# The last batch's routing and the first expert's token rows put in another order in an attention and mixture-of-experts kernel

## The chip, the cores and the metric

The kernel runs on one core of a Trainium2 chip. The metric is the device time of one execution in microseconds (us). The engines are PE (TensorE), DVE (VectorE), ACT (ScalarE), POOL (GpSimd) and SP (SyncE, which here only issues DMAs and loads numbers).

## The reference, cut to what matters

Attention with two masks gives rows of tokens; each row whose skip score is positive then goes through one of eight experts, the one with the largest gate logit.

```python
batch, n_heads, seq, head_dim = (8, 8, 576, 64)
N, D, E, F = (4608, 512, 8, 1024)
...
mask_local = (rel >= 0) & (rel < stride)
mask_strided = (rel >= 0) & (pos[None, :] % stride == pos[:, None] % stride)
masks = np.stack([mask_local if h < H // 2 else mask_strided for h in range(H)], axis=0)
...
return np.matmul(attn, v).astype(np.float32)
...
skip_score = x @ w_skip
do_compute = skip_score > 0
out = x.copy()
xc = x[do_compute]
logits = xc @ w_gate
e_idx = np.argmax(logits, axis=1)
...
for e in range(E):
    mask = e_idx == e
    h = np.maximum(xc[mask] @ w1[e], 0.0)
    y[mask] = gate_w[mask, None] * (h @ w2[e])
out[do_compute] = xc + y
```

## The kernel before

**Attention.** The work comes in 32 units, one for each batch (0 to 7) and quarter `pr` (0 to 3); the quarters 0 and 1 take the heads with the local mask, 2 and 3 the strided ones. The loop over the units stands under a manual schedule of POOL, PE, DVE and SP, so that these engines run what they are given in the order in which the code is written. Finished rows `x` are stored to `out` in DRAM.

**Routing.** Batches form groups (two and two first, then single ones). For each group `score` makes skip score and logits on PE (L381) and copies them to the tile `s9s` (four copies on ACT, L386). `route1` turns them (L400 on PE) and finds each token's expert: a chain on DVE (L408 to L423), the exponentials on ACT (L412), and on POOL the sums and the mask `rmk` of the tokens that are skipped (L428 to L432). `route2` gives each token its place in its expert's list: counting products on PE (L441 to L448), then DVE (L453 to L458, of which L457 needs `rmk`). `scat` writes these places by indirect DMAs on POOL into a `table` in DRAM (L470, five for a group of one batch). What is scattered waits in the list `sc_`. After the last group, `sort` and `places` count the experts' tokens (from L483 on PE, L488 to L543 on DVE) and leave the sorted numbers of the experts and their first rows in `order`.

**The experts.** Products are made of two float32r parts each (high `h`, low `l`), three products for one. The first expert, "e", is picked early, after batch 3, with 96 by 3 rows from batches up to 5. `rows` fetches its rows of the table into `tab` (a DMA, L638, on POOL or on SP), `gather` fetches the token rows `xg` from `out` (three indirect DMAs on POOL, L650), `xturn` turns them on PE (L675) and splits them on ACT (L677, `xh`) and DVE (L678, `xl`). `ffn1a` makes the hidden rows of the first two of eight blocks f (16 products with `xh`, L720, then eight with `xl`, L724), `ffn1` those of the others (L681 to L683), each block ended by `hout` (ACT L693, DVE L694). `ffn2` is the second layer: weights 0 to 3 of `w2` are called j 4 to 7, and its second half needs j 6 and 7. A weight tile comes by a DMA of 512 KB on SP (`wdma`, L596) into one of three `raw` tiles, is cast on ACT (L610) and its low part taken on DVE (L615).

Behind "e" come a leftover chunk "l" of 128 rows (turned at L675, products L788 to L815) and the other seven experts in sorted order, the first of which the code calls TURN[0]. Their table rows are read by `rows` on SP with numbers that SP loads out of `order` one by one. Which of two versions of the expert loop runs is decided by a branch on a number that `places` makes; the traced execution ran one. The transposes, the first products of "e", the routing of the last batch and the sorting stand in a manual schedule of PE, ACT and DVE; POOL and SP are ordered there by a scheduler.

Of the kernel before, what the change touches and what calls it, by code (L numbers as in the profile page):

```python
# [104 lines left out]
def attn_moe(ctx: ExitStack, tc: tile.TileContext, q, k, vl, vh, vs, w9d, w1d, w2d, cst, out, NB=B):  # L105
# [265 lines left out]
    def score(b, tag="T"):  # L371
# [13 lines left out]
        for h in range(4):  # L385
            A.copy(s9s[:, at + SQT * h:at + SQT * h + SQT], p[32 * h:32 * h + 9, 0:SQT])  # L386

# [451 lines left out]
    def run(*gs):  # L839
        weave(gs, [])  # L840
# [33 lines left out]
    for n, (b, pr) in enumerate(units):  # L874
# [86 lines left out]
        if b == CB + 2:  # L961
            if pr == 0:
                assert not sc_
            if pr == 1:
                rows("e", s0, *CE, eng=G)
            if pr == 3:
                gather("e", "e", "e", last=(CB + 1) * S)
    pool_order.close()
    nr = len(GROUPS) - 1
    with tc.manual_schedule(engines={T.engine, A.engine, V.engine}):  # L970
        run(pv(*units[-1]), xpose(*units[-2]), route2(ranked, of=CB))
        count(CB)
        run(xpose(*units[-1]), score(NB - 1), xturn("e"))
    while sc_:
        scat(*sc_.pop(0))
    for kind in range(2):
# [6 lines left out]
    ga = ffn1a("e")  # L983
    with tc.manual_schedule(engines={T.engine, A.engine, V.engine}):
        run(ga)
        wsplit("e", 3, 4)
        wdma("e", e0, 6, 7, st_["e"]["taken"])
        g = ffn1("e", 2, 6)
        run(islice(g, 4), later(route1, nr), islice(g, 4), later(route2, nr))
        while sc_:  # L990
            scat(*sc_.pop(0))
        wsplit("e", 4, 5)
        places = sort(NB - 1)
        run(g)
        judge, rest = places()
        actx.close()
        pool["b"] = ctx.enter_context(tc.tile_pool(name="bpool", bufs=1, reuse_waits="tile"))
        wsplit("e", 5, 6)
        run(ffn1("e", 6, 8))
    pctx.close()  # L1000
    psum, bufs = ctx.enter_context(tc.tile_pool(name="psumB", bufs=1, space=PSUM, reuse_waits="tile")), {"S": 4, "T": 2, "PV": 2}

    seq = [("e", e0, 6), ("e", e0, 7)]
    wdma(*seq[1], 8)
    s0n = G.value_load(isel[0:1, 2:3], min_val=0, max_val=(NE - 1) * ESTR + CE[0] * CE[1])
    rows("l", s0n, CT, 1, eng=G)
    slots = {}
    for r in TURN:
        e = nc.sync.value_load(order[0:1, 0, r:r + 1], min_val=0, max_val=NE - 1)
        seq += [(r, e, j) for j in range(8)]  # L1010
        if r == TURN[0]:
            wdma(*seq[2], 1)
        slots[r] = nc.sync.value_load(order[0:1, 1, r:r + 1], min_val=0, max_val=(NE - 1) * ESTR)
        if r == TURN[0]:
            assert SMALL[r] == CAPS[r]
            rows(r, slots[r], *CAPS[r])
    done = [0]

    def split():
        key, _, j = seq[done[0]]  # L1020
        wsplit(key, j, j + 1)
        done[0] += 1
        if done[0] + 2 < len(seq):
            wdma(*seq[done[0] + 2], seq[done[0] + 2][2] + 1)

# [28 lines left out]
    def experts(caps, tm):  # L1054
        last = ("e", CE[1])
        for r in TURN[1:]:
            rows(r, slots[r], *caps[r])
        with tc.manual_schedule(engines={T.engine, A.engine, V.engine, G.engine}):
            for i, r in enumerate(TURN):
                nxt = TURN[i + 1] if i + 1 < len(TURN) else None  # L1060
                if nxt is not None:
                    gather(nxt, "bbe"[(i + 1) % 3], "eh"[(i + 1) % 2])
                g = ffn1(r, 0, 8)
                for f in range(8):
# [114 lines left out]
```

## Time and profile before

| | us |
|---|---|
| median of three runs | 444.77 |
| lowest and highest | 444.13, 451.11 |
| the profiled execution | 448.78 |
| its span, first to last instruction | 447.1 |
| PE busy in it | 407.3 (91%) |
| DVE, ACT, POOL busy | 254.1, 192.8, 153.5 |

The profiled execution is 1.7 us longer than its span, and 4.0 above the median. Its mean granted clock of PE is 0.95 of full speed. An engine's busy time is an average over stages that differ: the attention fills the first 180 us, the experts the rest.

### The profile page before, as it was taken

How to read it: one execution, taken by the hardware profiler on the slowest of the kernel's cores; microseconds unless marked ns; L12 is line 12 of the kernel's file. 1: busy time of each engine (PE TensorE's matmuls, PEld its weight loads, DVE VectorE, ACT ScalarE, POOL GpSimd, SP SyncE). 2: the span in 40 equal slices, each digit the busy share in tenths (PEclk: the TensorE clock that was granted, in tenths of full speed). 3: DMA queues.
4: the chain of work that ended last, by engine and by line, in shares of the span. 5: the costliest groups of instructions: out<-in, count | busy, mean ns of one | idle time of the engine just before them, and what ended most of it. 6: DMA issues, size and time to landing. Idle time of an engine off the chain costs nothing. (4 is left out here: it accounts for less than half of the span.)

```text
span 447.1 us, 12291 instructions
## 1 busy us (share of the span) xinstructions
PE 407.3 (91%) x4995; PEld 365.0 (82%) x4996; DVE 254.1 (57%) x498; ACT 192.8 (43%) x372; POOL 153.5 (34%) x199
## 2 busy tenths in 40 slices
PE   6889998989898978599889999999999999999993
PEld 3778877677675856389779999999999998999973
DVE  4776774567765746265146546446457474757610
ACT  1556472536352715233253344345354454546500
POOL 2443435644748574424401441212202211321011
PEclk9989996999989868799989999999999999999998
DMA  8989998999979415714515866656547565685301
GB/s 270 370 287 296 305 326 181 257 268 271 247 204 286 134 59 139 216 48 96 170 58 160 226 200 180 190 150 199 190 142 227 169 202 173 196 285 162 119 21 46
DMA packets 47440, 86.36 MB, mean 193 GB/s; under 512 B 8095, under 2 KB 24735, under 8 KB 47374
## 3 DMA queue, kind: packets, MB, share of 16 engines
q1 hardware_dynamic: 41262, 75.32, 56.4%
q0 software_dynamic: 6112, 10.17, 7.6%
q8 instruction: 41, 0.67, 0.6%
q14 instruction: 25, 0.20, 0.2%
HBM read 70.44 MB, written 15.39 MB: 192 GB/s over the span
## 5 line engine op out<-in xcount | busy, mean ns | idle before, releaser
L681 PE MATMUL S<-xh,w1h 128*128 128x342 f32 (+5 forms) x248 | 76.6, 309 | 0.8 <-DVE hl L694 0.8
L761 POOL DMA_INDIRECT out_dram<-ot,tab x23 | 24.6, 1068 | 150.2 <-DVE ot L759 139.1
L682 PE MATMUL S<-xl,w1h 128*128 128x342 f32 (+5 forms) x248 | 75.1, 303 | 0.0
L683 PE MATMUL S<-xh,w1l 128*128 128x342 f32 (+5 forms) x248 | 75.0, 302 | 0.0
L681 PE MATMUL S<-hh,w2h 128*128 128x288 f32 (+4 forms) x160 | 50.1, 313 | 0.0
L693 ACT ACTIVATE hh<-S 128x342 fp32r<-128x342 f32 (+5 forms) x64 | 27.1, 425 | 52.9 <-PE S L683 40.7
L615 DVE TENSOR_TENSOR w1l<-raw,w1h 128x1024 fp32r<-128x1024 f32 x32 | 38.7, 1223 | 18.4 <-ACT w1h L610 17.2
L683 PE MATMUL S<-hh,w2l 128*128 128x288 f32 (+4 forms) x160 | 49.0, 306 | 0.0
L682 PE MATMUL S<-hl,w2h 128*128 128x288 f32 (+4 forms) x160 | 49.0, 306 | 0.0
L681 PEld LDWEIGHTS S<-xh,w1h 128*128 128x128 f32 x248 | 46.9, 189 | 1.6 <-DVE hl L694 1.3
L615 DVE TENSOR_TENSOR w2l<-raw,w2h 128x1024 fp32r<-128x1024 f32 x32 | 39.0, 1223 | 14.3 <-ACT w2h L610 10.1
L682 PEld LDWEIGHTS S<-xl,w1h 128*128 128x128 f32 x248 | 46.9, 189 | 0.2
L683 PEld LDWEIGHTS S<-xh,w1l 128*128 128x128 f32 x248 | 46.8, 189 | 0.0
L205 PE MATMUL S<-kt,qt 64*64 64x54 f32 (+1 forms) x1280 | 34.7, 250 | 8.9 <-DVE sm L223 3.2
L470 POOL DMA_INDIRECT table<-pay,rdi x38 | 38.7, 1018 | 10.7 <-issue 9.3
L205 PEld LDWEIGHTS S<-kt,qt 64*64 64x64 f32 x1280 | 28.7, 146 | 14.9 <-issue 8.4
L650 POOL DMA_INDIRECT xg<-out_dram,tab x23 | 27.9, 1215 | 34.1 <-DMA out_dram<-ot,tab 10.0
L232 POOL TENSOR_TENSOR sm<-sm,mx 128x384 f32<-128x384 f32 (+1 forms) x30 | 27.5, 939 | 33.3 <-DVE mx L229 17.9
L694 DVE SCALAR_TENSOR_TENSOR hl<-S,hh 128x342 fp32r<-128x342 f32 (+5 forms) x64 | 29.7, 468 | 16.0 <-ACT hh L693 15.1
L610 ACT CAST w2h<-raw 128x1024 fp32r<-128x1024 f32 x32 | 33.3, 1043 | 2.4 <-DMA raw<-in_w_dram 2.4
L678 DVE TENSOR_TENSOR xl<-T,xh 128x256 fp32r<-128x256 f32 (+6 forms) x30 | 12.6, 451 | 37.6 <-ACT xh L677 26.6
L610 ACT CAST w1h<-raw 128x1024 fp32r<-128x1024 f32 x32 | 33.3, 1060 | 0.0
(161 smaller groups left out, 857.8 us busy)
## 6 DMA issues: line engine op xcount, KB each, us to landing
raw<-in_w_dram SPq DMA_DIRECT2D x64, 512.0 KB
vt<-in_vs_dram SPq DMA_DIRECT2D x16, 390.0 KB
qt<-in_qp_dram SPq DMA_DIRECT2D x16, 304.0 KB
kt<-in_kp_dram SPq DMA_DIRECT2D x16, 297.0 KB
kt<-in_kp_dram SPq DMA_DIRECT2D x14, 304.0 KB
vt<-in_vl_dram SPq DMA_DIRECT2D x16, 260.0 KB
out_dram<-x SPq DMA_DIRECT2D x16, 256.0 KB
qt<-in_qp_dram SPq DMA_DIRECT2D x14, 288.0 KB
```

The costliest lines, as they stand in the source:

```text
L205: mark[0] = T.matmul(s[HP * (i ^ j):HP * (i ^ j) + HP, j, (blk - b0) * win:(blk - b0 + 1) * win], lhsT=qt[p, j, blk * nq:blk * nq + HP], r ...
L232: (V if b == kind == 0 and j else G).tensor_tensor(e[:, j], sw[:, j], mx[:, j].unsqueeze(2).broadcast_to([128, b1 - b0, win]), op=ALU.subt ...
L470: i = G.indirect_dma_start(out=table, out_offset=bass.IndirectOffsetOnAxis(ap=di[:, t:t + 1], axis=0), in_=pay[:, t, :], in_offset=None, b ...
L610: A.copy(hi, raw)
L615: V.tensor_tensor(lo, raw, hi.bitcast(F32), op=ALU.subtract)
L650: i = G.indirect_dma_start(out=xg[:s["P"], t, :], out_offset=None, in_=out[0:last, :], in_offset=bass.IndirectOffsetOnAxis(ap=s["tab"][:s[ ...
L681: T.matmul(p, lhsT=a[0], rhs=b[0], start=start, stop=False)
L682: T.matmul(p, lhsT=a[0], rhs=b[1], start=False, stop=False)
L683: T.matmul(p, lhsT=a[1], rhs=b[0], start=False, stop=stop)
L693: A.activation(s["hh"][:, f, :C], p[:, :C], AF.Relu)
L694: V.scalar_tensor_tensor(s["hl"][:, f, :C], p[:, :C], 0.0, s["hh"][:, f, :C].bitcast(F32), op0=ALU.max, op1=ALU.subtract)
L761: i = G.indirect_dma_start(out=out, in_=ot[:P], in_offset=None, bounds_check=NTOK - 1, oob_is_err=False, out_offset=bass.IndirectOffsetOnA ...
```

## The change

The four copies of the last batch's scores go to DVE. "e"'s token rows are gathered one unit sooner. POOL joins the manual schedules behind the loop. The last batch's `route1` comes between the two halves of "e"'s transposes, its `route2` between the products with `xh` and those with `xl`, and its scatters, the sorting and `places` come before and between the next blocks. TURN[0]'s table row is read on SP before the last two weight tiles of "e" are fetched, and the other experts' numbers are loaded by `load`, called where a weight tile or table row needs them.

```diff
 def score(b, tag="T"):
-            A.copy(s9s[:, at + SQT * h:at + SQT * h + SQT], p[32 * h:32 * h + 9, 0:SQT])
+            (A.copy if b + 1 < NB else V.tensor_copy)(s9s[:, at + SQT * h:at + SQT * h + SQT], p[32 * h:32 * h + 9, 0:SQT])
...
-            if pr == 3:
+            if pr == 2:
                 gather("e", "e", "e", last=(CB + 1) * S)
...
-    with tc.manual_schedule(engines={T.engine, A.engine, V.engine}):
+    with tc.manual_schedule(engines={T.engine, A.engine, V.engine, G.engine}):
         run(pv(*units[-1]), xpose(*units[-2]), route2(ranked, of=CB))
+        while sc_:
+            scat(*sc_.pop(0))
         count(CB)
-        run(xpose(*units[-1]), score(NB - 1), xturn("e"))
-    while sc_:
-        scat(*sc_.pop(0))
+        run(xpose(*units[-1]), score(NB - 1), xturn("e", 0, 2))
+        r1 = route1(nr)
+        next(r1)
+        run(xturn("e", 2, 4), r1)
...
-    with tc.manual_schedule(engines={T.engine, A.engine, V.engine}):
-        run(ga)
+    slots, es = {}, {}
+
+    def load(r, n):
+        x = nc.sync.value_load(order[0:1, n, r:r + 1], min_val=0, max_val=(NE - 1) * (1, ESTR)[n])
+        (es, slots)[n][r] = x
+
+    with tc.manual_schedule(engines={T.engine, A.engine, V.engine, G.engine}):
+        run(islice(ga, 8), later(route2, nr), ga)
+        while sc_:
+            scat(*sc_.pop(0))
+        places = sort(NB - 1)
+        g = ffn1("e", 2, 6)
+        run(islice(g, 4))
+        judge, rest = places()
+        load(TURN[0], 1)
+        assert SMALL[TURN[0]] == CAPS[TURN[0]]
+        rows(TURN[0], slots[TURN[0]], *CAPS[TURN[0]])
         wsplit("e", 3, 4)
         wdma("e", e0, 6, 7, st_["e"]["taken"])
-        g = ffn1("e", 2, 6)
-        run(islice(g, 4), later(route1, nr), islice(g, 4), later(route2, nr))
-        while sc_:
-            scat(*sc_.pop(0))
+        run(islice(g, 4))
         wsplit("e", 4, 5)
-        places = sort(NB - 1)
         run(g)
-        judge, rest = places()
...
-    seq = [("e", e0, 6), ("e", e0, 7)]
-    wdma(*seq[1], 8)
+    es["e"] = e0
+    seq = [("e", 6), ("e", 7)] + [(r, j) for r in TURN for j in range(8)]
+
+    def ahead(n):
+        key, j = seq[n]
+        if key not in es:
+            load(key, 0)
+        wdma(key, es[key], j, j + 1)
+
+    ahead(1)
     s0n = G.value_load(isel[0:1, 2:3], min_val=0, max_val=(NE - 1) * ESTR + CE[0] * CE[1])
     rows("l", s0n, CT, 1, eng=G)
-    slots = {}
-    for r in TURN:
-        e = nc.sync.value_load(order[0:1, 0, r:r + 1], min_val=0, max_val=NE - 1)
-        seq += [(r, e, j) for j in range(8)]
-        if r == TURN[0]:
-            wdma(*seq[2], 1)
-        slots[r] = nc.sync.value_load(order[0:1, 1, r:r + 1], min_val=0, max_val=(NE - 1) * ESTR)
-        if r == TURN[0]:
-            assert SMALL[r] == CAPS[r]
-            rows(r, slots[r], *CAPS[r])
+    ahead(2)
...
-        for r in TURN[1:]:
+
+        def fetch(r):
+            load(r, 1)
             rows(r, slots[r], *caps[r])
+
+        fetch(TURN[1])
         with tc.manual_schedule(engines={T.engine, A.engine, V.engine, G.engine}):
             for i, r in enumerate(TURN):
...
+                if i + 2 < len(TURN):
+                    fetch(TURN[i + 2])
```

**POOL, from the table rows of "e" to the scatters of batch 6's group.** L638 fetches the table rows, L650 gathers `xg`, L428 to L432 are `route1`'s and L470 the scatters. Before:

```order
L638 DMA tab<-table 96x12
L428 TENSOR_TENSOR rex<-rex 128x5x4
L428 TENSOR_TENSOR rex<-rex 128x5x2
L429 TENSOR_TENSOR rz<-rex 128x5
L430 TENSOR_SCALAR rz<-rz 128x5
L432 TENSOR_SCALAR rmk<-rmw 128x5
L650 DMA xg_3205<-out_dram,tab 96x512 x3
L470 DMA table<-pay_94,rdi 40960x4 x5
```

and now:

```order
L638 DMA tab<-table 96x12
L650 DMA xg_3126<-out_dram,tab 96x512 x3
L428 TENSOR_TENSOR rex<-rex 128x5x4
L428 TENSOR_TENSOR rex<-rex 128x5x2
L429 TENSOR_TENSOR rz<-rex 128x5
L430 TENSOR_SCALAR rz<-rz 128x5
L432 TENSOR_SCALAR rmk<-rmw 128x5
L470 DMA table<-pay_94,rdi 40960x4 x5
```

The three gathers stand ahead of that group's L428 to L432 instead of behind them. After these scatters follow, before and now, L428 to L432 of the last group, its five L470 and the reading of "l"'s table rows (L638).

**PE, from the last batch's scores to the first products of "e".** `xg` are the gathered rows, `s9s` the last batch's scores. Before:

```order
L381 MATMUL T<-xT_3101,w_65 32x144 x8
L381 MATMUL T<-xT_3243,w_65 32x144 x8
L675 MATMUL T<-cs,xg_3205 128x96 x12
L720 MATMUL S<-xh_3310,w1h_2859 128x288
L720 MATMUL S<-xh_3310,w1l_2863 128x288
```

and now:

```order
L381 MATMUL T<-xT_3243,w_65 32x144 x8
L675 MATMUL T<-cs,xg_3126 128x96 x6
L400 MATMUL T<-cs,s9s 128x9 x5
L675 MATMUL T<-cs,xg_3126 128x96 x6
L720 MATMUL S<-xh_3325,w1h_2859 128x288
L720 MATMUL S<-xh_3325,w1l_2863 128x288
```

The five L400, which stood behind block f=2, stand between two halves of the twelve L675. In the same way the counting products L441 to L448, which stood behind block f=3, now stand between the last L720 and the eight L724.

**SP, around the weight tiles j 6 and j 7 of "e".** raw_2550 and raw_2551 are the raw tiles that take them, raw_2552 the third (first j 5, then j 0 of TURN[0]); the names in brackets are the engines and DMA lanes whose semaphores the instruction waits for (DMASW: the indirect and other DMAs that POOL issued). Before:

```order
L596 DMA raw_2550<-in_w_dram 128x1024 [waits DMAHW7_49,DVE_49]
L596 ISA
L596 DMA raw_2551<-in_w_dram 128x1024 [waits DMAHW0_49,DVE_49]
L1009 TENSOR_LOAD order [waits DVE_49]
L1009 ISA x2
L596 ISA
L596 DMA raw_2552<-in_w_dram 128x1024 [waits DMAHW6_49,DMAHW1_49,DVE_49]
L1013 TENSOR_LOAD order
L1013 ISA x2
L638 ISA
L638 DMA tab<-table 114x12 [waits DMASW5_49,DMASW4_49,DMASW6_49,DMASW3_49,DMASW7_49,DMASW2_49,DMAHW2_49,DMASW1_49,DMASW0_49]
```

and now:

```order
L596 DMA raw_2552<-in_w_dram 128x1024 [waits DMASW7_49,DMASW6_49,DMAHW6_49,DMASW5_49,Activation_49]
L990 TENSOR_LOAD order [waits DVE_49]
L990 ISA x2
L638 ISA
L638 DMA tab<-table 114x12 [waits DMASW5_49,DMASW4_49,DMASW6_49,DMASW3_49,DMASW7_49,DMASW2_49,DMAHW7_49,DMASW1_49,DMASW0_49]
L596 ISA
L596 DMA raw_2550<-in_w_dram 128x1024 [waits DMAHW0_49,DVE_49]
L596 ISA
L596 DMA raw_2551<-in_w_dram 128x1024 [waits DMAHW1_49,DVE_49]
```

The read of TURN[0]'s table rows (L638), with its wait for the scatters, stands ahead of j 6 and j 7 instead of behind them. Further on, in the version of the expert loop behind the branch, the first two L638 are followed by ten loads of numbers in a row; before, all fourteen loads stood ahead of the branch.

## Rows read from the trace of the kernel before

**Rows 1.** Windows: busy us (instructions) per engine, PE clock, DMA share, GB/s.

```profile
184.10:190.80 6.70, 4.20 (x20) 3.90 (x21) 1.55 (x4) 2.39 (x8) 1.11 (x2) 0.50 0.53 134
225.10:228.40 3.30, 2.82 (x14) 2.82 (x15) 1.54 (x3) 2.03 (x4) 0.00 (x0) 0.50 0.00 0
240.00:430.00 190.00, 190.00 (x1289) 183.86 (x1288) 110.50 (x153) 86.85 (x148) 39.01 (x36) 1.00 0.61 184
```

**Rows 2.** Timeline of PE, 183 to 198: start, duration, instruction, idle before.

```profile
183.29 0.30 PE L675 MATMUL T<-cs,xg 96*128 96x96 f32 x1 [2.54 <-issue]
184.95 1.38 PE L675 MATMUL T<-cs,xg 96*128 96x96 f32 x7 [1.36 <-issue]
187.98 0.74 PE L675 MATMUL T<-cs,xg 96*128 96x96 f32 x3 [1.65 <-ACT s9s L386]
188.43 0.59 PE L720 MATMUL S<-xh,w1h 128*128 128x288 f32 x1
...
191.74 1.21 PE L724 MATMUL S<-xl,w1h 128*128 128x288 f32 x8
193.42 0.40 PE L681 MATMUL S<-xh,w1h 128*128 128x288 f32 x1 [0.47 <-DVE hl L694]
...
195.20 0.48 PE L400 MATMUL T<-cs,s9s 9*128 9x9 f32 x5
...
197.50 0.18 PE L441 MATMUL T<-rohb,tri 128*128 128x40 bf16 x1
...
197.99 0.38 PE L681 MATMUL S<-xh,w1h 128*128 128x288 f32 x1
```

**Rows 3.** Timeline of ACT, 180 to 206.

```profile
186.77 1.16 ACT L386 COPY s9s<-T 9x144 f32<-9x144 f32 x4 [7.24 <-PE T L675]
```

**Rows 4.** Timeline of POOL, 165 to 211.

```profile
174.44 1.10 POOL L650 DMA_INDIRECT xg<-out_dram,tab  x1 [0.58 <-issue]
175.84 1.97 POOL L650 DMA_INDIRECT xg<-out_dram,tab  x1 [0.30 <-issue]
...
179.38 1.01 POOL L470 DMA_INDIRECT table<-pay,rdi  x1 [0.30 <-issue]
...
184.54 0.97 POOL L470 DMA_INDIRECT table<-pay,rdi  x1 [0.30 <-issue]
196.99 0.53 POOL L428 TENSOR_TENSOR rex<-rex 128x20 f32<-128x20 f32 x2 [11.47 <-ACT rex L412]
...
199.56 1.76 POOL L470 DMA_INDIRECT table<-pay,rdi  x1 [1.08 <-DVE pay L458]
...
205.62 0.97 POOL L470 DMA_INDIRECT table<-pay,rdi  x1 [0.30 <-issue]
...
210.31 0.61 POOL L638 DMA_DIRECT2D tab<-table  x1 [3.71 <-DMA table<-pay,rdi]
```

**Rows 5.** Timeline of DVE, 165 to 206.

```profile
175.74 1.23 DVE L615 TENSOR_TENSOR w1l<-raw,w1h 128x1024 fp32r<-128x1024 f32 x1 [1.00 <-ACT w1h L610]
...
199.20 1.19 DVE L615 TENSOR_TENSOR w2l<-raw,w2h 128x1024 fp32r<-128x1024 f32 x1
```

**Rows 6.** Timeline of PE, 222 to 226.

```profile
222.24 0.32 PE L675 MATMUL S<-cs,xg 114*128 114x114 f32 x1 [0.46 <-DMA xg<-out_dram,tab]
225.58 0.45 PE L675 MATMUL S<-cs,xg 114*128 114x114 f32 x1 [3.03 <-DMA xg<-out_dram,tab]
```

**Rows 7.** Timeline of SP's DMA queue, 206 to 219.

```profile
209.78 0.35 SPq L638 DMA_DIRECT2D tab<-table  x1
217.46 1.33 SPq L596 DMA_DIRECT2D raw<-in_w_dram  x2
```

**Rows 8.** Timelines of SP's queue and of ACT, weight loads and their casts.

```profile
387.55 8.65 SPq L596 DMA_DIRECT2D raw<-in_w_dram  x5
...
391.21 1.05 ACT L610 CAST w2h<-raw 128x1024 fp32r<-128x1024 f32 x1 [1.50 <-DMA raw<-in_w_dram]
...
252.51 1.04 ACT L610 CAST w2h<-raw 128x1024 fp32r<-128x1024 f32 x1
```

More of the change, by code (lines that the diff above doesn't have):

```diff
@@ L1001, in attn_moe @@
     psum, bufs = ctx.enter_context(tc.tile_pool(name="psumB", bufs=1, space=PSUM, reuse_waits="tile")), {"S": 4, "T": 2, "PV": 2}
-    seq = [("e", e0, 6), ("e", e0, 7)]
-    wdma(*seq[1], 8)
+    es["e"] = e0
[6 more added lines that the diff above has]
+    ahead(1)
     s0n = G.value_load(isel[0:1, 2:3], min_val=0, max_val=(NE - 1) * ESTR + CE[0] * CE[1])
     rows("l", s0n, CT, 1, eng=G)
-    slots = {}
-    for r in TURN:
-        e = nc.sync.value_load(order[0:1, 0, r:r + 1], min_val=0, max_val=NE - 1)
-        seq += [(r, e, j) for j in range(8)]
-        if r == TURN[0]:
-            wdma(*seq[2], 1)
-        slots[r] = nc.sync.value_load(order[0:1, 1, r:r + 1], min_val=0, max_val=(NE - 1) * ESTR)
-        if r == TURN[0]:
-            assert SMALL[r] == CAPS[r]
-            rows(r, slots[r], *CAPS[r])
+    ahead(2)
     done = [0]
     def split():
-        key, _, j = seq[done[0]]
+        key, j = seq[done[0]]
         wsplit(key, j, j + 1)
@@ L1023, in split @@
         if done[0] + 2 < len(seq):
-            wdma(*seq[done[0] + 2], seq[done[0] + 2][2] + 1)
+            ahead(done[0] + 2)
     gather("l", "b", "h")
@@ L1089, in attn_moe @@
     small = nc.values_load(fits[0:1, 0:1], min_val=0, max_val=1)
-    live = [done, scats, reads, stores, wt, raw_, cast_, st_, turn]
-    kept = [list(x) for x in live[:4]] + [dict(x) for x in live[4:7]] + [{k: dict(x) for k, x in st_.items()}, dict(turn)]
+    live = [done, scats, reads, stores, wt, raw_, cast_, st_, turn, slots, es]
+    kept = [list(x) if isinstance(x, list) else {k: dict(y) if isinstance(y, dict) else y for k, y in x.items()}
+            for x in live]
     with tc.If(small > 0) as branch:
```

## The prediction

> **What bounds the kernel now.** PE is busy in 91% of the span, so the first view is the one of windows: from 240 to 430 us PE is busy in all 190.00 of 190 us at full clock [rows 1]. No edit gains anything there. The same view shows two stretches at a granted clock of 0.50, the lower of the two levels (1.2 of 2.4 GHz): 184.1 to 190.8, and 225.1 to 228.4 [rows 1]. Each lies behind a hole in PE's work, and PE's timeline shows what ended the hole.
>
> Hole 1: PE ends the last batch's scores and one transpose at 180.75 and does no L675 until 183.29, waits again before 184.95 and before 187.98, and starts L720 at 188.43 [rows 2]. The last wait is put down to ACT's copies of the scores, which began at 186.77 [rows 3] although the scores were done some six microseconds earlier. The two others carry no releaser. POOL's timeline names it: of the three gathers of "e" the second is issued at 175.84, the third between it and the scatters of 179.38 [rows 4], and what they fetch is what L675 turns.
>
> Hole 2: L675 of TURN[0] waits 0.46 and then 3.03 us for its gathered rows [rows 6]. The chain behind it is long: the last scatter is issued at 205.62, SP reads the table row when it has landed, at 209.78, POOL waits 3.71 for the same [rows 4, 7], and the gathers come after that. The head of the chain is the routing of the last batch, which starts at 195.20 (L400) and 197.50 (L441) among the products of "e" [rows 2].
>
> **Part 1: gathers and score copies.** In the new order the gathers stand ahead of L428 to L432 of batch 6's group and behind nothing that waits for routing; they can go some 4 us sooner, since the routing's chain on DVE and ACT is no longer ahead of them. They then land before the scores are done, so L675 waits for nothing but the copies. Four copies cost 1.16 on ACT [rows 3]; on DVE they are new, and I take 1.0 to 1.3 for them by that row. PE then has, from 180.45 (180.75 less one transpose of 0.30): six transposes of about 0.11 (the seven of 1.38 ran at half clock, 0.2 each [rows 2]), a wait for the copies to about 181.7, L400 with 0.48, six more transposes. L720 starts at about 182.8 in place of 188.43: **-5.6**. Of this about 1.5 is the wait for ACT's late copies, which may belong to this one execution; it is kept apart below.
>
> **Part 2: the clock.** The 16 L720 take 188.43 to 191.74, 3.3 us; at full clock the pitch is that of the eight L724, 1.21 for eight with the tail of the last [rows 2], near 0.13, so 2.1. Without the hole the clock shouldn't fall: **-1.2**.
>
> **Part 3: the routing moved ahead.** Its PE work only changes places: L400 0.48, and 0.49 from L441 to the next product at 197.99 [rows 2], with about 0.15 idle. That is 1.1 less in blocks f=2 to f=7, and it is spent again earlier: L400 is inside the 182.8, and L441 to L448 add 0.25 and about 0.4 of waiting for `rohb`, since DVE's chain of small operations comes behind four L678. L724 ends at 182.8 + 2.1 + 0.65 + 1.1 = 186.65. A wait is added on DVE: L457 needs POOL's `rmk`, and POOL does L428 to L432 of the last group only behind the five scatters of batch 6's, which it does until 184.54 + 0.97 = 185.5 [rows 4] as before, since DVE gives it their places at the same time. L428 to L432 take 196.99 to about 198.5, 1.5 us, so `rmk` is there at 187.05. Behind L457 on DVE stand the two L694 that let block f=2 begin: one reciprocal and one of about 0.5, so PE begins f=2 at 187.85. The wait is 1.2 where it was 0.47 [rows 2]. One more of 0.7 may come at f=5, behind a L615 of 1.2 [rows 5]. From 193.42 to the end of f=7 before (`ffn2` begins at 204.89 [rows 2]) are 11.45; now 11.45 - 1.1 = 10.3. So f=7 ends at 198.15 instead of 204.9, and parts 1 to 3 together give **-6.7**.
>
> **Part 4: the second hole.** The last scatters go out from 187.6; five take 5.1 (179.38 to 184.54 for the same number) and the last is issued at about 193 [rows 4]. Before, the last was issued at 205.62 and was in at 209.78, 4.2 later [rows 4, 7]; that gives 197.2, and 1 more if a L615 falls beside one of them, as it does below. Then come the table rows and four gathers, which begin at about 201 and are issued by 206; L675 wants them at 221.5 (222.24 less the wait of 0.46 and the one transpose before it [rows 6]) less 6.7, 214.8. Even the 6.9 that the last gather before took to land (the last of four that began behind the table rows of 210.31, issued by about 218.7, used at 225.58 [rows 4, 6]) fits. So the waits of 3.03 and 0.46 go: **-3.5**, and with them the stretch at half clock, where PE was busy 2.82 in 3.30 [rows 1]; half of that is **-1.4**.
>
> POOL and DVE get in each other's way here: the gather of 175.84 beside the L615 of 175.74 took 1.97 in place of about 1.0 [rows 4, 5], and the first of the last scatters 1.76 [rows 4]. In the new order one L615 falls among the last scatters, which costs up to 1 us of landing; phase 2 of `ffn2` feels at most half of that. The Trainium skill states the rule (SBUF — State Buffer, "SBUF: two separate sides"): a DVE operation with two SBUF inputs and a GpSimd operation share a port pair as an exclusive lock, and the one that comes second is blocked for the whole of the first. By it the 1.97 would be 2.1 (0.97 behind an L615 that ends at 176.97), so the trace nearly agrees; it speaks against placing the scatters where the weights are split, and the sum by it would be 0.1 worse.
>
> **Part 5: SP's queue.** TURN[0]'s table row, with its wait for the last scatters, now stands ahead of j 6 and j 7 of "e". Each later entry of this queue waits with it. A weight load that was waited for was cast 3.66 after its issue (387.55 to 391.21 [rows 8]); with a cast of 1.05 and a L615 of 1.2 that is 5.9 from issue to use. With the scatters in at 197.7, j 6 goes out at 198.5 and is usable at 204.4, j 7 at 205.5 or, if the two and the next share the DMAs, up to 2 later. The second half of `ffn2` begins 48 products of 0.133 behind f=7, 6.4 (211.25 before), so now at 204.55, and wants j 7 at 205.2. Bounds: 0 and 2.5 lost, **+0.8** taken, nearer the lower end, because one load alone fits. Below zero isn't possible, since before these two tiles were never waited for.
>
> The numbers loaded "when needed" come in fact ten in a row behind the branch. Before, twelve took 7.3 us less one DMA issue of 0.35 (209.78 to 217.46 [rows 7]), 0.6 each. Behind the branch SP then spends about 8.5 us (twelve loads, two reads of table rows) in place of 3.6 (six reads, the last just ahead of 245.01), so the next weight tile goes out 4.9 later. It was issued at 245.01 and cast at 252.51 [rows 8], 3.8 more than the 3.66 that a load takes. Bounds: 0 and 1.1, **+0.3** taken. Taking the twelve loads from ahead of the branch gains nothing by itself: nobody waited for SP there but the weight tiles of TURN[0], which are covered.
>
> **The sum.** -6.7 - 3.5 - 1.4 + 0.8 + 0.3 = -10.5 against the profiled execution: 448.78 to 438.3. That execution is 4.0 above the median of 444.77, and I can't say where its 4.0 lie; the wait for the copies (1.5) may be a part. So against the median I take -9 to -11.6 and in the middle **-10: 434.8 us**. Two per cent, about what a measurement of this kernel can tell from no change, is 8.9 us: the line is at 435.9.
>
> **Rivals.** (a) *Only the first hole closes fully.* What speaks for it: j 6, j 7 and TURN[0]'s first tile now go out one behind the other just when the four gathers do, and before the last gathers took 6.9 to land beside two such loads. Against it: 1 to 8 us of slack for the gathers. If 2 more is lost in phase 2 and half of hole 2 with its clock stays, it is 434.8 + 2 + 2 = 438.8, 437 to 441, within 2%. The holding of DVE by L457, if POOL's `rmk` comes later than 187.05, costs the same kind of microseconds. (b) *The slower side: SP's wait for the scatters.* Every microsecond that the scatters land after 197.2 goes to the second half of `ffn2` once j 6 is late; 11 later, at about 208.7, all gains are gone, and 20 later it is slower by 2%, 454. For it: the wait is on all of POOL's DMA lanes and nothing goes past it. Against it: nothing in the trace made a scatter land more than 4.2 behind its issue. (c) *The change doesn't do what it says:* the numbers aren't loaded when needed but ten in a row, and if the tile of TURN[0] has no cover, the full 4.9 comes on the path: 439.7. The cast at 252.51, not waiting for its tile [rows 8], speaks against it. (d) *More than forecast:* the median's execution has the two holes as wide as the profile, and no phase-2 wait follows: 444.77 - 11.6 - 1.5 = 431.7.
>
> **How the numbers follow.** Forecast (433.2 to 436.4) 0.52, (a) 0.27, (c) 0.07, (d) 0.10, (b) 0.04. Faster by over 2%: most of the forecast's 0.52 (0.46) and (d): 0.56; within: 0.40; slower: 0.04. The range of 431.5 to 440.5 takes in the forecast, (d), (c) and most of (a).
>
> **What would show it.** In the changed profile: gathers of "e" issued before 174, L675 at 180.5 without a wait for gathered rows, L720 at about 182.8 with a granted clock near 1.00 in what follows; DVE L457 waiting for POOL L432 at about 187; last scatter at about 193; SP's L638 at 197 to 198, L681 of `ffn2` waiting for L615 by no more than 2 us near 205; no wait of L675 for TURN[0]'s rows. The prediction is wrong if the first hole is filled by another wait (rmk, s9s on DVE), if the half clock stays, or if j 6 and j 7 are late by more than 2.5.

## The result and the profile after

| | before | changed |
|---|---|---|
| median of five runs | 444.77 | 440.23 |
| lowest and highest | 443.24, 451.11 | 438.75, 443.04 |
| the profiled execution | 448.78 | 443.04 |
| its span | 447.1 | 441.4 |

The ratio is 0.990 (0.985 to 0.995): 4.5 us by the medians, in place of the 10 of the forecast. The two profiled executions, 4.0 and 2.8 above their medians, lie 5.7 apart in place of 10.5. So the question is which terms of the sum stayed out. (Experiment 4's profile below was taken in an execution 1.7% longer than that kernel's fastest, and is left out of the tables.)

The prediction leans on three places of the trace of before that its rows don't show, the start of L381 of the last batch, of `ffn2` and of TURN[0]'s first product, and on one issue in SP's queue. Timeline of PE, kernel before:

```profile
178.87 1.65 PE L381 MATMUL T<-xT,w 128*32 128x144 f32 x32
...
205.00 0.30 PE L681 MATMUL S<-hh,w2h 128*128 128x288 f32 x1
...
237.40 0.32 PE L681 MATMUL S<-xh,w1h 128*128 128x342 f32 x1
```

Timeline of SP's queue, kernel before:

```profile
245.01 16.18 SPq L596 DMA_DIRECT2D raw<-in_w_dram  x5
```

(`ffn2` begins at 205.00; the prediction's 204.89 is 0.1 early.) Timeline of PE after, the rows that answer to [rows 2, 6] and to those just shown; start, duration, instruction, idle before it:

```profile
179.66 2.15 PE L381 MATMUL T<-xT,w 128*32 128x144 f32 x32
181.74 0.89 PE L675 MATMUL T<-cs,xg 96*128 96x96 f32 x6
185.07 1.38 PE L400 MATMUL T<-cs,s9s 9*128 9x9 f32 x5 [2.45 <-issue]
...
187.31 0.59 PE L720 MATMUL S<-xh,w1h 128*128 128x288 f32 x1
...
191.56 1.67 PE L724 MATMUL S<-xl,w1h 128*128 128x288 f32 x8
...
193.70 0.40 PE L681 MATMUL S<-xh,w1h 128*128 128x288 f32 x1 [0.45 <-DVE hl L694]
...
204.40 0.30 PE L681 MATMUL S<-hh,w2h 128*128 128x288 f32 x1
...
220.46 0.46 PE L675 MATMUL S<-cs,xg 114*128 114x114 f32 x3
...
231.07 0.32 PE L681 MATMUL S<-xh,w1h 128*128 128x342 f32 x1
```

The differences of these starts split the two executions into stretches. The forecast's column is from the points that the prediction names (L720 182.8, L724 185.55, f=2 187.85, f=7's end 198.15, then its terms of -4.9, +0.8 and +0.3):

| stretch | before | forecast | after |
|---|---|---|---|
| start to L381 of the last batch | 178.87 | 178.87 | 179.66 |
| L381 to the first L720 | 9.56 | 3.93 | 7.65 |
| L720 to L724 | 3.31 | 2.75 | 4.25 |
| L724 to f=2 | 1.68 | 2.30 | 2.14 |
| f=2 to `ffn2` | 11.58 | 10.30 | 10.70 |
| `ffn2` to TURN[0]'s first product | 32.40 | 28.30 | 26.67 |
| from there to the end of the span | 209.7 | 210.0 | 210.3 |

The second hole is gone, and with it more than was forecast: the three L675 at 220.46 stand without a wait where [rows 6] has 0.46 and 3.03. The first hole is not: 1.9 of its 5.6 came. And behind it PE is at half clock as before. Windows of after (busy us and instructions of PE, PEld, DVE, ACT, POOL, then the granted clock, the DMA share and GB/s):

```profile
187.00:192.00 5.00, 5.00 (x29) 4.85 (x28) 2.85 (x12) 1.28 (x4) 1.16 (x5) 0.50 0.36 104
...
219.00:231.00 12.00, 12.00 (x82) 10.75 (x81) 5.52 (x8) 7.33 (x12) 0.00 (x0) 1.00 0.25 83
```

The second of these lines answers to the 0.50 of 225.1 to 228.4 in [rows 1]: full clock and no idle time.

In the first hole L675 no longer waits for gathered rows; what ended last there was another thing. Timeline of POOL after, answering to [rows 4]:

```profile
164.52 0.60 POOL L638 DMA_DIRECT2D tab<-table  x1
168.25 1.04 POOL L650 DMA_INDIRECT xg<-out_dram,tab  x1 [3.13 <-DMA tab<-table]
...
170.86 0.96 POOL L650 DMA_INDIRECT xg<-out_dram,tab  x1 [0.30 <-issue]
...
179.75 1.10 POOL L470 DMA_INDIRECT table<-pay,rdi  x1 [6.42 <-DVE pt L513]
...
185.01 0.97 POOL L470 DMA_INDIRECT table<-pay,rdi  x1 [0.30 <-issue]
...
190.60 0.26 POOL L432 TENSOR_SCALAR rmk<-rmw 128x5 f32<-128x5 f32 x1
...
198.26 1.23 POOL L470 DMA_INDIRECT table<-pay,rdi  x1 [0.30 <-issue]
...
203.44 1.24 POOL L650 DMA_INDIRECT xg<-out_dram,tab  x1 [1.56 <-PE S L683]
```

Timeline of DVE after, answering to [rows 5]:

```profile
184.72 1.30 DVE L386 COPY s9s<-T 9x144 f32<-9x144 f32 x4 [4.42 <-remote]
...
192.47 0.17 DVE L457 TENSOR_TENSOR rdi<-rds,rmk 128x5 int32<-128x5 f32 x1 [0.27 <-DVE rds L455]
```

Timeline of ACT after, answering to [rows 3]:

```profile
184.82 0.40 ACT L677 CAST xh<-T 128x288 fp32r<-128x288 f32 x1 [4.60 <-remote]
186.98 1.06 ACT L677 CAST xh<-T 128x288 fp32r<-128x288 f32 x3 [1.76 <-remote]
```

The gathers are issued before 174, as forecast, and their rows are there. But DVE's score copies begin at 184.72, 2.9 after the scores ended at 181.81 (179.66 + 2.15), and ACT's first L677 at 184.82, 2.2 after the six L675 it reads (181.74 + 0.89); the profile finds nothing on the core that ended just before and writes "remote". L400, which reads the copies, starts after an idle time of 2.45. All this while POOL issues the scatters of batch 6's group, from 179.75 to 185.98. So the late copies of [rows 3], which the prediction took for ACT's and perhaps for one execution's, came back on DVE.

### The profile page after: what moved, and what is told of

Same layout as the page of the kernel before. It is cut to its first block, busy times and chain, and to the rows that moved or that the text cites. A ratio compares the mean times of both kernels' runs of the same rounds, so it can differ in the third digit from the quotient of the medians.

```text
span 441.4 us, 12283 instructions
## 1 busy us (share of the span) xinstructions
PE 407.6 (92%) x4995; PEld 365.0 (83%) x4996; DVE 256.4 (58%) x502; ACT 191.8 (43%) x368; POOL 152.9 (35%) x199
## 5 line engine op out<-in xcount | busy, mean ns | idle before, releaser
L615 DVE TENSOR_TENSOR w1l<-raw,w1h 128x1024 fp32r<-128x1024 f32 x32 | 38.7, 1223 | 18.6 <-ACT w1h L610 17.8
L615 DVE TENSOR_TENSOR w2l<-raw,w2h 128x1024 fp32r<-128x1024 f32 x32 | 39.2, 1225 | 14.2 <-ACT w2h L610 12.6
L470 POOL DMA_INDIRECT table<-pay,rdi x38 | 38.3, 1008 | 17.9 <-issue 8.8
L650 POOL DMA_INDIRECT xg<-out_dram,tab x23 | 27.8, 1208 | 37.6 <-DMA out_dram<-ot,tab 11.5
L205 PE MATMUL S<-kt,qt 64*64 64x54 f32 (+1 forms) x1280 | 32.5, 242 | 7.4 <-DVE sm L223 3.7
L694 DVE SCALAR_TENSOR_TENSOR hl<-S,hh 128x342 fp32r<-128x342 f32 (+5 forms) x64 | 29.7, 468 | 15.1 <-ACT hh L693 14.1
L205 PEld LDWEIGHTS S<-kt,qt 64*64 64x64 f32 x1280 | 26.6, 140 | 12.8 <-issue 5.5
L260 ACT ACTIVATE ptl<-T 96x512 f32<-96x512 f32 (+1 forms) x40 | 19.7, 547 | 29.8 <-PE T L252 21.0
```

Source lines behind the costliest of these rows:

```text
L205: mark[0] = T.matmul(s[HP * (i ^ j):HP * (i ^ j) + HP, j, (blk - b0) * win:(blk - b0 + 1) * win], lhsT=qt[p, j, blk * nq:blk * nq + HP], r ...
L470: i = G.indirect_dma_start(out=table, out_offset=bass.IndirectOffsetOnAxis(ap=di[:, t:t + 1], axis=0), in_=pay[:, t, :], in_offset=None, b ...
L615: V.tensor_tensor(lo, raw, hi.bitcast(F32), op=ALU.subtract)
L650: i = G.indirect_dma_start(out=xg[:s["P"], t, :], out_offset=None, in_=out[0:last, :], in_offset=bass.IndirectOffsetOnAxis(ap=s["tab"][:s[ ...
L694: V.scalar_tensor_tensor(s["hl"][:, f, :C], p[:, :C], 0.0, s["hh"][:, f, :C].bitcast(F32), op0=ALU.max, op1=ALU.subtract)
```

## The experiments

On the chips where the experiments ran the kernel before takes 427 to 429 us, and PE reaches the last batch's L381 at 156 to 161 in place of 179. Experiments 1 to 8 ran on one such chip, 9 to 12 on another. Each ratio is to runs of the kernel before that were taken with it (medians 427.72 for 1 to 4, 428.72 for 5 to 8, 426.73 for 9 to 12).

My theory after the result: the gathered rows land late because the DMA engines are nearly full around the last scores (0.84 busy in the first hole before, 0.72 after), and the gathers can't start as early as I took. Rivals: the scatters on POOL and their DMAs hold PE up; or the hole is chance, another width in every execution.

The stretches of all profiled executions, worked out as above, and where in front of L381 (minus) or behind it the things of the first hole lie ("third gather ends" is its start and duration in POOL's timeline).

| kernel | L638 issued | third gather ends | L381 to L720 | L720 to L724 | f=2 to `ffn2` | `ffn2` to TURN[0] | TURN[0] to end |
|---|---|---|---|---|---|---|---|
| before | -11.9 | +0.2 | 9.56 | 3.31 | 11.58 | 32.40 | 209.7 |
| changed | -15.1 | -7.8 | 7.65 | 4.25 | 10.70 | 26.67 | 210.3 |
| 9 before again | -7.4 | 0.0 | 6.11 | 3.73 | 11.56 | 32.3 | 210.3 |
| 7 before, stores later | -8.0 | -0.2 | 3.87 | 2.33 | 11.56 | 34.0 | 209.7 |
| 5 changed again | -10.6 | -3.1 | 4.38 | 2.65 | 10.28 | 26.8 | 211.2 |
| 1 no scatters | -7.0 | -1.1 | 7.71 | 3.99 | 10.27 | 26.7 | 210.7 |
| 2 stores later | -9.7 | -1.4 | 4.88 | 3.83 | 10.27 | 26.8 | 214.9 |
| 3 gathers at the old place | -7.5 | -0.2 | 9.39 | 3.76 | 10.28 | 26.8 | 210.8 |
| 6 loads ahead | -9.0 | -3.1 | 4.97 | 3.93 | 10.30 | 26.8 | 209.7 |
| 8 = 2 and 6 | -6.9 | -1.1 | 6.14 | 4.25 | 10.27 | 26.8 | 211.0 |
| 10 TURN[0]'s row last | -7.3 | -1.1 | 7.86 | 3.98 | 10.31 | 26.8 | 210.9 |
| 11 table rows on SP | -9.1 | -2.7 | 4.64 | 2.64 | 10.29 | 26.8 | 211.0 |
| 12 = 8 and 11 | -8.6 | -2.3 | 4.80 | 3.93 | 10.28 | 26.8 | 210.1 |

**1. No scatters of batch 6's group.**

```diff
-        while sc_:
-            scat(*sc_.pop(0))
+        sc_.clear()
         count(CB)
```

> The changed kernel without the five scatters of batch 6's group (their tokens get no expert; nothing else is left out). Theory A (PE gets its instructions and posts its semaphores late while POOL's indirect DMAs run): PE's hole between the last batch's scores and L400 (2.45 us in the changed kernel) falls below 0.5, L720 starts within 4.0 us of the start of the last L381 in place of 7.65, the clock stays near 1.00 in the L720, and the time is 2.5 to 5 us below the changed kernel's 440.2, 435 to 438. Theory B (the nine stores of the last batch's rows fill the DMA engines and delay the semaphores): the hole stays at 2 to 3 us and the time within 1 us of the changed kernel's. Theory C (DVE's copies of the scores are slow to begin for a reason on DVE): the hole stays as well.

Measured 421.45, 0.990 (0.985 to 0.995). The hole is there without any scatter in it. Timeline of PE, experiment 1:

```profile
158.13 1.66 PE L381 MATMUL T<-xT,w 128*32 128x144 f32 x32
...
163.46 0.90 PE L675 MATMUL T<-cs,xg 96*128 96x96 f32 x4 [1.83 <-DMA xg<-out_dram,tab]
...
165.84 0.59 PE L720 MATMUL S<-xh,w1h 128*128 128x288 f32 x1
```

Timeline of POOL, experiment 1:

```profile
153.38 1.03 POOL L650 DMA_INDIRECT xg<-out_dram,tab  x1 [1.68 <-DMA tab<-table]
...
155.99 1.09 POOL L650 DMA_INDIRECT xg<-out_dram,tab  x1 [0.30 <-issue]
```

L675 waits for gathered rows, the thing that the change was to have ready. On this chip the hole needs no scatters: 7.71 to L720 without them. It says nothing of the late starts in the result's profile, since no profile of the experiments has any, with scatters or without.

**2. The stores of the last batch's rows held back to the first L720.**

```diff
-    for kind in range(2):
-        for part in jobs_out(NB - 1, kind):
-            issue(part)
...
         run(islice(ga, 8), later(route2, nr), ga)
+        for kind in range(2):
+            for part in jobs_out(NB - 1, kind):
+                issue(part, begun[0].ins)
```

(`begun` lists the L720.)

> The changed kernel with the nine stores of the last batch's rows held until the first L720 (nothing left out). Theory B (these stores cause the hole): the hole in front of L400 falls below 0.5, L720 within 4.0 us of the start of the last L381, time 435 to 438. Theory A (the scatters of batch 6's group cause it): the hole stays at 2 to 3 us, L720 7 to 8 us behind that L381, and the time is that of the changed kernel within 1.5 us, 439 to 441.5.

Measured 421.75, 0.988 (0.982 to 0.993). L381 to L720 takes 4.88, between the values that the two theories gave. The profile's last stretch holds a late gather of the expert loop near 376, 2.25 of idle time on PE; experiments 8 and 9 have 1.1 and 0.3 at the same place, the others none. It is no part of the change's working.

**3. The gathers back at the old place, all else changed.**

```diff
-            if pr == 2:
+            if pr == 3:
                 gather("e", "e", "e", last=(CB + 1) * S)
```

> The changed kernel with the gathers of the first expert where they were before, one unit later (nothing left out). Theory A (indirect DMAs slow PE wherever they run beside many small products): the stretch from the start of batch 6's L381 to that of batch 7's L381 goes from 15.1 back to about 11.8, L675 waits for rows 2 to 4 us, and the time is within 1.5 us of 440.2. The prediction's theory (the gathers of the first expert are what hole 1 waits for): hole 1 opens again to the 9.6 us from L381 to L720 of before and nothing comes back ahead of it: 442 to 444.

Measured 423.08, 0.990 (0.986 to 0.994). The widest hole of the experiments, 9.39, with L675 waiting 0.71 and 3.57 for rows, and yet the gain of the change within the interval.

**4. The gathers alone**, in the kernel before: its `if pr == 3` becomes `if pr == 2`, the opposite of 3.

> The kernel before with only one part of the change: the first expert's gathers one unit sooner (nothing left out). Theory A: from batch 6's L381 to batch 7's L381 14 to 15 us in place of 11.8, L381 to L720 7 to 8 in place of 9.6, together 1 to 2 us slower or the same: 444 to 447. The prediction's theory: L381 to L720 4 to 5 in place of 9.6, and 439 to 441.

Measured 425.98, 0.999 (0.996 to 1.003). By 3 and 4 the earlier gathers are worth nothing that these runs resolve, and the gain of about a per cent comes from the rest.

**5. The changed kernel again**, unaltered.

> The changed kernel itself, to see on one chip with the next three which of its waits return. Theory D (hole 1 is time in which the DMA engines are full of the last stores, and the gathered rows or what PE waits for land late wherever the gathers stand): L381 of batch 7 to the first L720 again 7.3 to 7.9 us, against 9.4 to 9.6 before. Theory E (the hole in the first trace of the changed kernel was an accident of that execution): 4.5 to 5.5 us. Either way the stretch from batch 6's L381 to batch 7's is 11.3 to 12.5 us and not 15.1, and ffn2 to the next expert's first product 26.7.

Measured 420.82, 0.985 (0.978 to 0.993). In this execution the hole nearly closed. Timeline of POOL, experiment 5:

```profile
150.34 0.60 POOL L638 DMA_DIRECT2D tab<-table  x1
154.19 1.03 POOL L650 DMA_INDIRECT xg<-out_dram,tab  x1 [3.25 <-DMA tab<-table]
...
156.80 0.96 POOL L650 DMA_INDIRECT xg<-out_dram,tab  x1 [0.30 <-issue]
```

Timeline of PE, experiment 5:

```profile
160.90 2.12 PE L381 MATMUL T<-xT,w 128*32 128x144 f32 x32
...
163.75 0.55 PE L675 MATMUL T<-cs,xg 96*128 96x96 f32 x4 [0.41 <-DMA xg<-out_dram,tab]
...
165.28 0.38 PE L720 MATMUL S<-xh,w1h 128*128 128x288 f32 x1
```

The table rows were asked for 10.6 ahead of L381 here, 7.0 ahead in experiment 1; the code in front of L638 is the same. POOL waited 3.25 for them, then the gathers went, and their rows came 0.41 late. With the gathers at the new place the hole is 7.71, 4.38 and, in the result's profile, 7.65: what differs between executions is part of it.

**6. All numbers loaded ahead, behind TURN[0]'s.**

```diff
     ahead(2)
+    for r in TURN[1:]:
+        load(r, 0)
+        load(r, 1)
...
         def fetch(r):
-            load(r, 1)
             rows(r, slots[r], *caps[r])
```

> The changed kernel with the twelve other numbers loaded ahead of the branch, as before the change (nothing left out). If the ten loads in a row behind the branch make the weight tile j 7 of the next expert late, the wait of L683 for L615 (0.7 us) goes, and the time from that expert's first product to the end is 209.7 to 209.9 us, as before the change, in place of 210.3 to 210.8. If not, the wait stays. In the time 0.5 to 1 us, which three rounds can't tell.

Measured 422.04, 0.988 (0.981 to 0.996), no better than 5 in time. In the profile the last stretch is 209.7 in place of 211.2. The row that goes, from the timeline of PE of experiment 5 (TURN[0]'s second layer):

```profile
227.31 0.42 PE L683 MATMUL S<-hh,w2l 128*128 128x342 f32 x1 [0.68 <-DVE w2l L615]
```

Experiments 1, 2, 3, 5, 10 and 11 have this wait of 0.6 to 0.7, and 6, 8 and 12, which load ahead, don't; nor does the old order (7, 9).

**7. The kernel before with its stores held back**, the edit of 2.

> The kernel before, with only the nine stores of the last batch's rows held until the first L720 (nothing left out). Theory D: L381 of batch 7 to the first L720 falls from 9.5 to 6 to 8 us, since the gathered rows land faster although the gathers stand where they did. Theory E and the prediction's theory (the place of the gathers alone sets it): 9 to 10 as before. The second hole stays in both; it may grow by 1 to 2, since the last rows reach the DRAM later.

Measured 425.73, 0.994 (0.990 to 0.998). The narrowest first hole of all, with the gathers at their old place. Windows from L381 to L720 and on to L724, experiment 7:

```profile
157.85:161.72 3.87, 3.59 (x46) 2.49 (x45) 0.53 (x5) 2.10 (x8) 2.98 (x3) 0.75 0.37 109
161.72:164.05 2.33, 2.33 (x18) 2.32 (x17) 1.53 (x4) 0.85 (x3) 1.94 (x2) 1.00 0.97 97
```

Timeline of POOL, experiment 7:

```profile
149.86 0.59 POOL L638 DMA_DIRECT2D tab<-table  x1 [0.15 <-issue]
150.62 0.51 POOL L428 TENSOR_TENSOR rex<-rex 128x20 f32<-128x20 f32 x2 [0.17 <-ACT rex L412]
...
153.20 1.10 POOL L650 DMA_INDIRECT xg<-out_dram,tab  x1 [1.11 <-DMA tab<-table]
154.61 1.73 POOL L650 DMA_INDIRECT xg<-out_dram,tab  x1 [0.31 <-issue]
```

L428 to L432 (1.5 us) are over before the table rows have come: in this execution they stood in a wait that was there anyway, and the gathers gain by leaving them behind only what is left of it. The DMA share in the hole is 0.37, and L720 to L724 runs at full clock.

**8. Stores held back and loads ahead**, the edits of 2 and 6.

> The changed kernel with both: the nine stores held until the first L720 and the numbers loaded ahead of the branch (nothing left out). Theory D: L381 to L720 4.5 to 5.5 us, no wait for j 7, and 2 to 4 us less than the changed kernel on the same chip. Theory E: no difference beyond 1 us.

Measured 419.89, 0.981 (0.975 to 0.987). In its profile the hole is 6.14 although the stores are out of the way: L638 went out only 6.9 ahead of L381. 4.5 to 5.5 were expected.

**9. The kernel before again**, unaltered.

> The kernel before itself, one look at its trace on a chip on which PE is not seen to post late (nothing left out). Theory D (the third gather of the first expert ends near the start of batch 7's L381 and its rows land 6 to 7 us later while the last stores fill the DMA engines): L381 to L720 9 to 10 us, L675 waiting for rows at about 6 to 7 us behind L381, with the score copies begun at about 2. Theory E (the hole of the first traces was an accident): below 6.

One run, 423.1. Timeline of POOL, experiment 9:

```profile
148.34 0.59 POOL L638 DMA_DIRECT2D tab<-table  x1
148.95 0.56 POOL L428 TENSOR_TENSOR rex<-rex 128x20 f32<-128x20 f32 x2
...
151.41 1.10 POOL L650 DMA_INDIRECT xg<-out_dram,tab  x1 [0.95 <-DMA tab<-table]
152.81 1.70 POOL L650 DMA_INDIRECT xg<-out_dram,tab  x1 [0.30 <-issue]
154.81 0.96 POOL L650 DMA_INDIRECT xg<-out_dram,tab  x1 [0.30 <-issue]
```

Timeline of PE, experiment 9:

```profile
155.78 2.15 PE L381 MATMUL T<-xT,w 128*32 128x144 f32 x32
...
160.36 0.31 PE L675 MATMUL T<-cs,xg 96*128 96x96 f32 x1 [2.08 <-DMA xg<-out_dram,tab]
161.07 1.04 PE L675 MATMUL T<-cs,xg 96*128 96x96 f32 x10 [0.40 <-DMA xg<-out_dram,tab]
161.89 0.39 PE L720 MATMUL S<-xh,w1h 128*128 128x288 f32 x1
...
199.18 0.32 PE L675 MATMUL S<-cs,xg 114*128 114x114 f32 x1 [3.04 <-DMA xg<-out_dram,tab]
```

The old order's hole was 6.11 here, not 9.56: L428 doesn't wait for the routing's chain, which it did for 4.73 in the profile of before, and there is no late copy. The second hole is there with its old size, 3.04.

**10. TURN[0]'s table row read behind the weight tiles again.**

```diff
-        load(TURN[0], 1)
-        assert SMALL[TURN[0]] == CAPS[TURN[0]]
-        rows(TURN[0], slots[TURN[0]], *CAPS[TURN[0]])
...
     ahead(2)
+    load(TURN[0], 1)
+    assert SMALL[TURN[0]] == CAPS[TURN[0]]
+    rows(TURN[0], slots[TURN[0]], *CAPS[TURN[0]])
```

> The changed kernel with the table row of the second expert read behind the weight tiles j 6, j 7 and j 0, as before the change; the routing stays early (nothing left out). If the early routing alone closes the second hole: from the first product of ffn2 to the second expert's first product 26.7 to 27.3 us, as in the changed kernel, and the time within 1 us of it. If reading the row first is what closes it: L675 waits for rows again, 1 us or more, and that stretch is 28 us or more.

Measured 421.36, 0.988 (0.982 to 0.994). `ffn2` to TURN[0] takes 26.8 and L675 doesn't wait. The routing ahead of the products closes the second hole by itself; reading the row first adds nothing that shows.

**11. "e"'s table rows read on SP, in unit 0 in place of unit 1.**

```diff
-            s0 = G.value_load(isel[0:1, 1:2], min_val=0, max_val=(NE - 1) * ESTR)
+            s0 = nc.sync.value_load(isel[0:1, 1:2], min_val=0, max_val=(NE - 1) * ESTR)
...
-            if pr == 1:
-                rows("e", s0, *CE, eng=G)
+                rows("e", s0, *CE)
```

> The changed kernel with the first expert's table rows read on SP at the end of unit (7,0) in place of on POOL behind the masks of the later units (nothing left out). Theory D: the gathers were held by the reading of these rows (POOL waits 3 to 4 us for them), so now the third gather ends 4 to 6 us ahead of batch 7's L381, its rows land at its start or soon after, L381 to L720 falls to 3.9 to 4.5 us with the clock near 1.00 in every execution, and the time is 0 to 2 us below the changed kernel's. If the gathers' place on POOL alone sets them: no change, 4.4 to 7.7.

Measured 419.56, 0.984 (0.978 to 0.989). POOL's wait in front of the gathers is now 1.47, and for the stored rows (`out_dram<-x`), not for the table. The third gather ends 2.7 ahead of L381 where 4 to 6 were expected, and the hole is 4.64, not 3.9 to 4.5.

**12. The edits of 2, 6 and 11 together.**

> The changed kernel with all three: the first expert's table rows read on SP, the nine last stores held until the first L720, the numbers loaded ahead of the branch (nothing left out). Theory D: L381 to L720 3.9 to 4.5 us at full clock, no wait for j 7, time ratio to the kernel before 0.978 to 0.985, the fastest of all.

Measured 418.42, 0.980 (0.975 to 0.984): the fastest kernel here, and the only one whose upper end is clear of 0.985. The ratio is the one expected; the hole isn't: 4.80 and a granted clock of 0.57 behind it, where 3.9 to 4.5 at full clock were expected. Against the changed kernel itself it wasn't run on one chip; against experiment 10, on the same chip, it is 418.42 to 421.36, with intervals that overlap.

## Why the prediction was wrong, step by step

The time lies at the upper end of the range, and the forecast move was twice the one measured. No rival had this case: (a) has the first hole closed and the second half open, and it came the other way round, so that its 437 to 441 holds the measured 440.23 by accident. Two of the prediction's own signs of being wrong came: the first hole was filled by the wait for `s9s` on DVE, and the half clock stayed. (Rival (d) counts the 1.5 of the late copies twice, since its 11.6 holds them already in part 1's 5.6; without that it ends at 433.2.)

**Part 1 is the step that failed**: "they can go some 4 us sooner ... so L675 waits for nothing but the copies", with the copies done at about 181.7: -5.6. In the profile of the result the gathers did come in time (ended 7.8 ahead; no wait of L675). The term that was mis-sized there is the wait for the copies. They begin at 184.72, so that L400 starts 5.4 behind L381 where the forecast has 2.8; and L400 and the second six L675, partly at half clock (granted 0.61), take 2.2 to L720 where it has 1.1. These 2.6 and 1.1 are the 3.7 that the first hole fell short. The prediction had set "the wait for ACT's late copies, which may belong to this one execution" (1.5) apart and given it to ACT. But the late start of what reads PE's results was there in both profiles of the result, on ACT and then on DVE, 2.9 behind the scores after, and in none of the others: in experiments 5 and 9 the copies began 2.2 and 2.3 after L381's start, as it ended. Moving the copies from ACT to DVE was no cure for it. Its cause stays open; the last section has what the record says of it.

In the experiments part 1 failed by two other things. That the hole was a wait for gathered rows, which the prediction had inferred where the profile names no releaser, is named in experiment 9 (2.08 and 0.40). The first is what kept the gathers. In the profile of before it was the routing's chain on DVE and ACT, and I took that for the rule. In experiments 3, 7 and 9, also with the gathers at the old place, L428 waits 0.2 or less for it; behind L432 POOL waits for the table rows (1.11 in 7, 0.95 in 9), and with the new place it waits for them the longer (1.7 in experiment 1, 3.25 in 5, 3.13 after). The third gather ended 1.1 to 3.1 ahead of the scores in place of 0.2 ahead to 0.2 behind: 0.8 to 3.3 sooner, not 4. The second is the landing, which the prediction didn't price ("They then land before the scores are done"). From the end of the third gather's issue to the L675 that waited for its rows were 6.0 (experiment 5), 6.4 (1) and 5.3 (9), and 5.3 to 7.3 in all seven profiles with the stores in place. Rows issued 1.1 ahead and 6.4 under way come 3 to 4 behind scores that take about 2, and so the hole stays. In the experiments where the table rows went out 9 or more ahead of L381 (2, 5, 6, 11) it was 4.4 to 5.0, near the forecast's 3.93; in those with 7.5 or less (1, 3, 8, 9, 10) 6.1 to 9.4.

What sets the time at which L638 goes out against the scores, -6.9 to -15.1 with the same code ahead of it in all but 11 and 12, was not found. My theory of full DMA engines is only half borne out. With the stores held back the rows were under way for 3.0 to 5.5 (DMA engines 0.37 to 0.76 busy in the hole), with the stores in place for 5.3 to 7.3 (0.75 to 0.89). But the holes are 3.87, 4.80, 4.88 and 6.14 in the one case and 4.38 to 9.39 in the other, since the start of the gathers also counts: experiments 5 and 1 are 3.3 apart, 2.1 of it by the time at which the third gather ended and 0.4 by the landing. Held stores make the old order 0.6% faster (7, 0.2 to 1.0%), but 2 can't be told from 5 in time.

**Part 2**, the clock, hung on part 1. Of the rows of L720 to L724 those with L381 to L720 of up to 4.64 took 2.33 to 2.65 (three kernels), those with 4.80 or more 3.31 to 4.25 (all others), and the windows show 1.00 for the one and 0.50 to 0.63 for the other. In the changed profile it was 0.50 and 4.25: where 0.56 was to come, 0.94 was lost, as the moved L441 to L448 also run at half clock there.

**Part 3** was right where it could be seen: f=2 to `ffn2` 10.27 to 10.31 in every changed kernel of the experiments (10.3 forecast), 10.70 in the result's profile, with two waits of 0.35 and 0.23. The wait of DVE for POOL's `rmk`, taken as 1.2 ahead of f=2, wasn't paid: L432 is done at 190.9, L457 runs at 192.47 behind DVE's own L455, and f=2 waits 0.45 for L694. L428 to L432 got their turn behind the scatters early enough, since all of DVE's chain came later.

**Part 4** was right and too small. The last scatter goes out at 198.26 (forecast 193, but with f=2 5.9 later than forecast), SP reads the table rows at 200.80, POOL's gathers begin at 203.44, and PE has no wait at 220.46. -5.7 in place of -4.1 with part 5's share, and 26.7 to 26.8 in all ten profiles with the routing moved, 32.3 and more in the three of the old order.

**Part 5**: the +0.8 for j 6 and j 7 was not paid at all. Timeline of SP's queue after, answering to [rows 7]:

```profile
200.80 0.34 SPq L638 DMA_DIRECT2D tab<-table  x1
201.74 26.63 SPq L596 DMA_DIRECT2D raw<-in_w_dram  x7
```

Timeline of ACT after, answering to [rows 8]:

```profile
205.29 1.05 ACT L610 CAST w2h<-raw 128x1024 fp32r<-128x1024 f32 x1 [0.27 <-DMA raw<-in_w_dram]
206.53 1.05 ACT L610 CAST w2h<-raw 128x1024 fp32r<-128x1024 f32 x1 [0.19 <-DMA raw<-in_w_dram]
...
248.61 1.05 ACT L610 CAST w2h<-raw 128x1024 fp32r<-128x1024 f32 x1 [2.32 <-DMA raw<-in_w_dram]
```

j 6 and j 7 are cast 3.6 and 4.8 after the first issue at 201.74, and the second one's low part is wanted 6.4 behind the start of `ffn2`, at 210.8. With a cast of 1.05 and a L615 of 1.2 it is ready at 208.8: 2 us in hand. The scatters were in 2.5 after the last one's issue (198.26 to 200.80) and not 4.2, and that issue lay 6.1 ahead of `ffn2`, not 5.2. The +0.3 for the ten loads of numbers was the right mechanism and somewhat small: the cast at 248.61 waits 2.32 for its tile, and the last stretch is 0.55 longer than before (209.75 and 210.30), though PE has no wait there that the profile shows; on the other chips PE waits 0.6 to 0.7 there, and loading ahead takes it away. (Experiment 9, of the old order, has 210.3 too, so the stretch alone would prove nothing.)

The sum: the first hole and its clock fell short by 3.7 and 1.5, the start of the last batch's scores was 0.8 later (batch 6's began 2.5 earlier than before, and from there it took 15.1, where the other profiles have 11.5 to 13.8; why was not found), f=2 on 0.2 net and the end 0.25 worse, and the second hole gave 1.6 more. 3.7 + 1.5 + 0.8 + 0.2 + 0.25 - 1.6 = 4.85, and between the forecast of 438.3 and the profiled 443.04 lie 4.7; the rest is the 0.1 by which the prediction had `ffn2` early.

The sentence on the lock of the Trainium skill (SBUF — State Buffer, "SBUF: two separate sides") spoke against scatters among the L615. For a DVE operation with two SBUF inputs the page has the lock only against a GpSimd operation that reads SBUF; gathers and scatters read their row numbers there (`tab`, `rdi`). After, four of the last five scatters take 0.98 to 1.07 and the one beside an L615 1.23, so it cost 0.3 where the prediction allowed 1. The second gather beside an L615 took 1.70 and 1.73 in experiments 9 and 7 and 0.97 in 5 without: the trace agrees, each time about 0.1 short of the rule.

## What to carry to other kernels

One profile shows which of two waits ended last in one execution. Before an instruction's release is priced at the whole of a wait, look for the next one behind it (here the table rows, then the DMA's landing) and subtract what it takes. In the experiments the moved gathers were worth 1 to 3 us of start and nothing measurable in time. What held in every run was the move of a whole chain from its head (routing, scatters, table rows, gathers): no execution has a wait at its end any more. Where a stretch differs by several us between executions, a hole in it is priced from two or three profiles of the kernel before, not from one.

## What the runs showed of the hardware

In the two profiles of the result PE reaches the last batch's scores 18 to 24 us later than in those of the experiments (178.87 and 179.66, against 155.8 to 160.9), and from TURN[0] on the times are equal (209.7 and 210.3, against 209.7 to 211.2, but for experiment 2). In the views of waits of these two profiles ACT and DVE have five and six waits with the releaser "remote", up to 6.6 us in one; those of the experiments have none. All eleven end while POOL issues a group's scatters (L470) or at most 1.0 behind the last of them, and so, 1.3 behind, do the late copies of [rows 3]. That PE's results reach their readers late while POOL issues indirect DMAs is thus a rival that the record leaves standing for that chip, and no more than a coincidence in time: in experiment 5 the same scatters run (from 160.97) and the copies begin at 163.10, as the scores end. No experiment was made on a chip that shows these waits, so what the engines wait for stays open.

An indirect DMA of 96 rows took 5.3 to 7.3 us from the end of its issue to the use of its rows with the last stores beside it, and 3.0 to 5.5 with these held back. When its issue began and how long it was under way both set the first hole of the experiments.
